# Storing the three pieces of the last output tile through ScalarE's queue

## The chip, the cores and the metric

One core of one Trainium2 chip. The metric is the device time of one execution in microseconds (us). The kernel before takes 906.08 us, the median of 3 runs (905.79 to 906.3). All runs told here are fast, at a granted TensorE clock of 0.998 to 1.000.

## The reference

The program computes `x + s * g` for 2048 rows of 640 columns, in bfloat16. `s` is an attention over the last 512 of 2048 keys with 32 heads of 192, projected back by `wo`; `g` is a gated layer. Cut to what matters:

```python
def reference(A_x, A_k_cache, A_v_cache, A_wq, A_wo, B_x, B_w_gate, B_w_up, B_w_down):
    # ... _A_ref: q = x @ wq, softmax over the last 512 keys, o @ wo
    # ... _B_ref: (sigmoid(x @ w_gate) * (x @ w_up)) @ w_down
    xn = _layernorm(x, axis=-1)
    s = _A_ref(xn, A_k_cache, A_v_cache, A_wq, A_wo)
    g = _silu(_B_ref(xn, B_w_gate, B_w_up, B_w_down))
    return x + s * g
```

## The kernel before

The heads are worked off in groups. In the last group each tile of 128 output rows is finished: a product with the last slice of `wo` in PSUM, a multiply by the gate, an add of everything gathered so far, and a store to HBM. Only this end matters here.

```python
    def finish(ps, gB_sb, t, d0, d1, on_pool=False):
        o_sb = late["fout"].tile([P, D], BF16, name="o_sb")   # a pool of 4 buffers
        d = slice(d0, d1)
        if on_pool:
            tmp = late["tmp"].tile([P, D], F32, name="tmp")
            nc.vector.tensor_tensor(tmp[:, d], ps, gB_sb[:, d], ALU.mult)
            nc.gpsimd.tensor_tensor(o_sb[:, d], tmp[:, d], acc[t][:, d], ALU.add)
        else:
            nc.vector.tensor_tensor(ps, ps, gB_sb[:, d], ALU.mult)
            nc.vector.tensor_tensor(o_sb[:, d], ps, acc[t][:, d], ALU.add)
        nc.sync.dma_start(of[t * P:(t + 1) * P, d], o_sb[:, d])

    def stage_wo(r, i, q):
        # ...
        if r == last and i * TQ + q == 2 * TQ - 1:             # the last tile
            cuts = [0, D // 2, D - P, D]                       # pieces of 320, 192, 128 columns
            for e, (d0, d1) in enumerate(zip(cuts, cuts[1:])):
                ps = ps_all[:, (4, 5, 0)[e], 0:d1 - d0]
                wo_mm(ps, r, i, q, [(d0, d1 - d0)], d0)
                finish(ps, gates[t], t, d0, d1)
            return
        # ... the other tiles; the one before the last is finished with on_pool=True
```

So the add of the tile before the last runs on GpSimd, those of the three pieces on VectorE, and all stores are issued by the SP engine ("sync") in program order.

The softmax here doesn't subtract the row's maximum and nothing guards it: scores larger than these inputs give would overflow.

## Time and profile before

| | us |
|---|---|
| time (median) | 906.08 |
| span of the profiled run | 904.37 |
| last matmul ends | 898.65 |
| VectorE's adds of the pieces a, b, c end | 898.88, 899.55, 900.20 |
| their stores leave SP | 900.03, 900.50, 901.29 |
| their stores have landed | 901.68, 902.06, 903.27 |
| from c's landing to the end | 1.09 |

Three readings are worth learning before the prediction's lines. A store has two times: the issue, which the timeline shows on the sequencer that issues it (`SPq`, `ACTq`), and the landing, when the last of the sixteen DMA engines has reported; the trace records each of the sixteen reports. An instruction's wait is over when its semaphore reaches its value, which the trace also records; an instruction that starts much later than that was held by something else. And the queues in the page tell who issued what:

```profile
q1 hardware_dynamic: 159088, 57.85, 32.2%
q10 hardware_dynamic: 19488, 11.41, 5.3%
q8 instruction: 61, 1.00, 0.5%
q14 instruction: 24, 0.20, 0.1%
```

These are the queue's packets, megabytes and share of the DMA engines' time. q10 holds exactly ScalarE's issues (28 loads of 192 KB and 6 of 960 KB make 11.4 MB), so q1 is SP's; q8 and q14 bring instructions.

### The profile page before, as it was taken

To read this page: it belongs to the slowest core of one execution; us is meant where nothing else is said; L and a number is where in the kernel's file an instruction comes from. 1 tells how busy PE (TensorE), PEld (TensorE's weight loads), DVE (VectorE), ACT (ScalarE), POOL (GpSimd) and SP (SyncE) were. 2 spreads that over 40 slices of the span, in tenths; PEclk is the share of its full clock that TensorE was granted. 3 is DMA by queue.
4 is the path that set the end of the run, shared out by engine and by line. 5 is a ranking of instruction groups with operands and counts; after the bars stand their busy time and mean duration, and the time that the engine had idled before them with its cause. 6 is when DMAs were issued, how large, how long until landed. Compare 5 with 4: busy or idle time off the path is not lost.

```text
span 904.4 us, 18474 instructions
## 1 busy us (share of the span) xinstructions
PE 890.9 (99%) x7711; PEld 530.8 (59%) x7791; DVE 652.3 (72%) x1090; ACT 433.0 (48%) x511; POOL 179.3 (20%) x220
## 2 busy tenths in 40 slices
PE   8999999999999999999999999999999999999997
PEld 5545454556656565656565656565666666666664
DVE  4879956677677866785778677867786678666566
ACT  4323346764247533753375337643764285424240
POOL 0051212780001100110011001100110000002972
PEclk9999999999999999999999999999999999999999
DMA  9993374415544545364626362727293715264744
GB/s 280 271 265 95 97 146 104 119 54 87 86 91 68 135 78 99 60 143 69 109 60 143 62 115 52 151 54 123 36 167 50 126 34 117 48 111 147 155 120 114
DMA packets 188069, 100.38 MB, mean 111 GB/s; under 512 B 156176, under 2 KB 180368, under 8 KB 187984
## 3 DMA queue, kind: packets, MB, share of 16 engines
q1 hardware_dynamic: 159088, 57.85, 32.2%
q0 software_dynamic: 9408, 29.93, 14.0%
q10 hardware_dynamic: 19488, 11.41, 5.3%
q8 instruction: 61, 1.00, 0.5%
q14 instruction: 24, 0.20, 0.1%
HBM read 57.87 MB, written 5.24 MB: 70 GB/s over the span
## 4 chain that ended last, share of the span: by engine, by line
PE 96%; issue 1%; DVE 1%; DMA 1%; ACT 0%; SPq 0%; POOL 0%; DVEq 0%; POOLq 0%
PE ps_all L714 22%; PE ps_all L563 20%; PE ps_all L671 19%; PE ps_all L653 18%; PE ps_all L447 11%; PE ps_all L497 6%; PE ps_all L360 1%; DMA x_sb<-in_A_x_dram 0%; DVE qT L601 0%; ACT E L657 0%; DVE raw L221 0%; DMA out_dram<-o_sb 0%; POOL o_sb L726 0%; SPq L297 0%; DVE stats L324 0%
## 5 line engine op out<-in xcount | busy, mean ns | idle before, releaser
L657 ACT ACTIVATE E<-ps_all 128x1024 bf16<-128x1024 f32 x256 | 252.9, 1022 | 302.8 <-PE ps_all L653 255.5
L714 PE MATMUL ps_all<-wo_g,oT 128*128 128x128 bf16 (+2 forms) x1479 | 225.0, 295 | 3.3
L653 PE MATMUL ps_all<-qT,kT 64*128 64x512 bf16 x1536 | 194.4, 376 | 0.0
L671 PE MATMUL ps_all<-v_sb,E 128*128 128x193 bf16 x2048 | 189.8, 247 | 0.1
L671 PEld LDWEIGHTS <-E 128*128 128x128 bf16 x2048 | 168.6, 98 | 18.7 <-issue 6.8
L714 PEld LDWEIGHTS <-oT 128*128 128x128 bf16 x1542 | 121.5, 98 | 78.3 <-issue 2.1
L584 DVE COPY qp<-ps_all 128x512 f32<-128x512 f32 x150 | 100.7, 688 | 58.5 <-PE ps_all L563 58.4
L601 DVE TENSOR_TENSOR qT<-ps_all,qp 128x512 bf16<-128x512 f32 x165 | 109.6, 687 | 45.7 <-PE ps_all L563 37.4
L653 PEld LDWEIGHTS <-kT 64*128 64x128 bf16 x1536 | 75.3, 94 | 89.4 <-issue 5.2
L678 DVE TENSOR_TENSOR o_st<-ps_all,rden 128x768 bf16<-128x768 f32 x120 | 114.9, 957 | 5.0 <-DMA oT<-o_st 0.9
L202 POOL DMA_DIRECT2D raw<-in_A_wq_dram x80 | 48.5, 611 | 274.0 <-ACT wB L224 237.6
L135 POOL DMA_DIRECT2D k_sb<-in_A_k_cache_dram x32 | 32.7, 1027 | 276.3 <-DVE o_st L678 155.7
L219 ACT ACTIVATE raw<-raw,w_sc 128x1536 f16<-128x1536 bf16 x37 | 58.3, 1575 | 1.4 <-DMA raw<-in_A_wq_dram 0.5
L497 PE MATMUL ps_all<-wd_sb,hT_sb 128*128 128x128 bf16 (+1 forms) x377 | 52.4, 298 | 0.4
L563 PE MATMUL ps_all<-XA,wA 64*128 64x512 f16 x420 | 51.9, 376 | 0.2 <-DVE qp L584 0.2
L563 PE MATMUL ps_all<-XB,wB 64*128 64x512 f16 x420 | 52.0, 376 | 0.0
L563 PE MATMUL ps_all<-X,w 64*128 64x512 bf16 x420 | 51.9, 376 | 0.0
L749 DVE TENSOR_TENSOR acc_lo<-ps_all,acc_lo 128x640 f32<-128x640 f32 x48 | 39.4, 822 | 15.2 <-PE ps_all L714 15.1
L453 DVE TENSOR_TENSOR hT_sb<-ps_all,sig_sb 128x512 bf16<-128x512 f32 x48 | 32.4, 682 | 21.7 <-ACT sig_sb L452 11.4
L677 DVE RECIPROCAL rden<-ps_all 128x4 f32<-128x4 f32 x128 | 23.1, 180 | 33.5 <-PE ps_all L671 32.3
L452 ACT ACTIVATE sig_sb<-ps_all 128x512 bf16<-128x512 f32 x48 | 28.0, 596 | 39.8 <-PE ps_all L447 36.7
L749 DVE TENSOR_TENSOR acc_hi<-ps_all,acc_hi 128x640 f32<-128x640 f32 x48 | 39.3, 818 | 7.8 <-PE ps_all L714 7.8
(118 smaller groups left out, 761.6 us busy)
## 6 DMA issues: line engine op xcount, KB each, us to landing
raw<-in_A_wq_dram POOLq DMA_DIRECT2D x80, 192.0 KB, 3.8
k_sb<-in_A_k_cache_dram POOLq DMA_DIRECT2D x32, 192.0 KB, 5.9
wo_g<-in_A_wo_dram ACTq DMA_DIRECT2D x6, 960.0 KB, 6.8
v_sb<-in_A_v_cache_dram ACTq DMA_DIRECT2D x28, 192.0 KB, 3.7
gB_d<-gB_sb POOLq DMA_DIRECT2D x16, 160.0 KB, 4.2
gBa_sb<-gB_d SPq DMA_DIRECT2D x16, 160.0 KB, 3.8
xa_sb<-in_A_x_dram SPq DMA_DIRECT2D x16, 160.0 KB, 3.8
out_dram<-o_sb SPq DMA_DIRECT2D x15, 160.0 KB, 1.8
```

Of the source, the lines that this page charges most:

```text
L219: nc.scalar.activation(raw.bitcast(F16), raw, AF.Copy, scale=w_up)
L447: nc.tensor.matmul(gu[:, i, :], lhsT=w[:, c, f * P:(f + 1) * P], rhs=xnT[s][:, c, :], start=(c == 0), stop=(c == NCD - 1),)
L497: nc.tensor.matmul(oB_ps[:, d0:d0 + dsz], lhsT=hT_sb[:, f, q * P:(q + 1) * P], rhs=wd_sb[:, f, d0:d0 + dsz], start=(f == 0), stop=(f == NF ...
L563: nc.tensor.matmul(ps_all[:, b, :], lhsT=w(r, c), rhs=x[r, c, :], start=(first and k == 0), stop=(k == len(cs) - 1), skip_group_check=True,)
L584: nc.vector.tensor_copy(dst, part(b))
L601: nc.vector.tensor_tensor(q_out(i, u, pp), part(b), t, ALU.add)
L653: nc.tensor.matmul(ps[:, b, :], lhsT=kT[h, c * PC + j, :], rhs=qT_t[r][i, j][h, pp, :], start=(j == 0), stop=(j == PC - 1),)
L657: nc.scalar.activation(E_t[r, i, pp][:, c, :, :], ps, AF.Exp, scale=scale_qk)
L671: nc.tensor.matmul(o_ps[:, q // 2, q % 2, 0:DH + 1], lhsT=E[:, c, h, q * P:(q + 1) * P], rhs=vt[:, c, 0:DH + 1], start=(c == 0), stop=(c = ...
L678: nc.vector.tensor_tensor(o_st[:, :, h * DH:(h + 1) * DH].rearrange("p (b i) d -> p b i d", b=2), o_ps[:, :, :, 0:DH], rden[:].to_broadcas ...
L714: nc.tensor.matmul(oA[:, d0 - base:d0 - base + dsz], lhsT=oT_t[r, i, pp][:, q * PC + j, :], rhs=wo_t[runs[r][1]][:, cc, d0:d0 + dsz], star ...
L749: nc.vector.tensor_tensor(acc[t][:], oA[:, 0:D], acc[t][:], ALU.add)
```

## The change

Its intent is to let the three last stores leave by a queue that has nothing else to do at the end, instead of standing behind the store of the tile before.

```diff
-    def finish(ps, gB_sb, t, d0, d1, on_pool=False):
+    def finish(ps, gB_sb, t, d0, d1, on_pool=False, queue=nc.sync):
 ...
-        nc.sync.dma_start(of[t * P:(t + 1) * P, d], o_sb[:, d])
+        queue.dma_start(of[t * P:(t + 1) * P, d], o_sb[:, d])
 ...
-                finish(ps, gates[t], t, d0, d1)
+                finish(ps, gates[t], t, d0, d1, queue=nc.scalar)
```

## The prediction

> **What bounds the kernel now.** I read the page first, then the chain that ended last, then the timeline of the last seven microseconds, the waits of the DMA queue's own sequencer there, and the issues with their times to landing.
>
> ```profile
> span 904.4 us, 18474 instructions
> PE 890.9 (99%) x7711; PEld 530.8 (59%) x7791; DVE 652.3 (72%) x1090; ACT 433.0 (48%) x511; POOL 179.3 (20%) x220
> PE 96%; issue 1%; DVE 1%; DMA 1%; ACT 0%; SPq 0%; POOL 0%; DVEq 0%; POOLq 0%
> ...
> out_dram<-o_sb SPq DMA_DIRECT2D x15, 160.0 KB, 1.8
> ```
>
> TensorE is busy for 99% of the span and makes 96% of the chain. Nothing in the change touches it, so the body of 898 us stays as it is. What can move is the end, after the last matmul. There the timeline shows this:
>
> ```profile
> 897.66 0.99 PE L714 MATMUL ps_all<-wo_g,oT 128*128 128x192 bf16 x12
> 898.01 1.54 POOL L726 TENSOR_TENSOR o_sb<-tmp,acc_hi 128x640 bf16<-128x640 f32 x1
> 898.39 0.49 DVE L729 TENSOR_TENSOR o_sb<-ps_all,acc_hi 128x320 bf16<-128x320 f32 x1
> 899.19 0.36 DVE L729 TENSOR_TENSOR o_sb<-ps_all,acc_hi 128x192 bf16<-128x192 f32 x1
> 899.91 0.29 DVE L729 TENSOR_TENSOR o_sb<-ps_all,acc_hi 128x128 bf16<-128x128 f32 x1 [0.16 <-DVE ps_all L728]
> ...
> 897.95 0.33 SPq L730 DMA_DIRECT2D out_dram<-o_sb  x1
> 899.58 0.33 SPq L730 DMA_DIRECT2D out_dram<-o_sb  x1
> 900.03 0.35 SPq L730 DMA_DIRECT2D out_dram<-o_sb  x1
> 900.50 0.39 SPq L730 DMA_DIRECT2D out_dram<-o_sb  x1
> 901.29 0.33 SPq L730 DMA_DIRECT2D out_dram<-o_sb  x1
> ```
>
> First two columns: start and duration in us. TensorE ends at 898.65. Call the three pieces of the last tile a (320 columns), b (192) and c (128). Their adds end at 898.88, 899.55 and 900.20. The stores come out much later: the SP sequencer takes them in program order, so it first waits for GpSimd's add of the tile before (ends 898.01 + 1.54 = 899.55), issues that store at 899.58, and only then a at 900.03, b at 900.50 and c at 901.29. Piece a waits 1.15 us behind a store that it has nothing to do with, b 0.95, c 1.09.
>
> ```profile
> SPq L730 <- POOL o_sb L726: 3.2, 2, 2.0
> SPq L861 <- DMA out_dram<-o_sb: 1.2, 1, 1.2
> ...
> out_dram<-o_sb SPq DMA_DIRECT2D x1, 80.0 KB, 1.6
> out_dram<-o_sb SPq DMA_DIRECT2D x1, 48.0 KB, 1.6
> out_dram<-o_sb SPq DMA_DIRECT2D x1, 32.0 KB, 2.0
> ```
>
> The first line is SP held by GpSimd; the second is the closing wait of the program, 1.2 us, for the landing of c (issue 901.29 + 1.98 = 903.27). From there the closing barrier runs to 904.37: 1.10 us. So the end is: c's add 900.20, 1.09 us of queueing, 1.98 us of transfer, 1.10 us of closing = 904.37.
>
> **What the Trainium skill says.** "DMA: Bandwidth & Descriptors", section "Issuing engines are not separate DMA queues": transfers of all issuing engines run on the same 16 DMA engines, and issuing from several saves only sequencer time, "usually small". The trace agrees so far that sequencer time is all there is to win, but here it is on the path: 1.09 us in front of the last store.
> "Perfetto Trace Analysis", section "DMA Instruction — HWDGE (DVE, Sync)": the descriptor generator is locked for one sequencer at a time, inside the profiled issue. ScalarE's 28 loads of v took 547 ns min and median, 649 at most, though many ran beside a transpose of SP; so sharing cost them 0.1 us at worst.
> "Runtime: NRT & Kernel Launch", section "Instruction fetch mechanics": an engine's instructions come in blocks of 256. I compared every SP record with the moment its semaphores were satisfied. Only two started more than 0.15 us after it: SP's record 79 (0.23 us) and record 335 (0.34 us), exactly 256 apart, each followed 0.6 us later by one 8 KB packet of the instruction queue that took 540 ns. Record 335 is the store of c. So 0.34 of its 1.09 us looks like a block boundary, and the trace agrees with the page.
> The same DMA page, "Anatomy of one DMA — SWDGE (gpsimd) path", puts the fixed cost of a transfer at about 2 us, mostly the write receipt. The trace has 1.57 to 1.98 us for 32 to 160 KB, nearly flat in size; no queue will shorten it.
>
> **The change, part by part.** Removed from SP: three issues with their semaphore waits (six records). Added to ScalarE: the same six, after its last exponential, which ended at 871.0; ScalarE has nothing else to do. On TensorE, VectorE and GpSimd the order of instructions is the same, and each store keeps its waits. Nothing is removed from the data movement.
>
> Piece a: ScalarE can issue it at 898.91 (add's end + 0.03 us, the reaction that SP shows after GpSimd: 899.55 to 899.58). It lands near 900.6, no longer on the path.
> Piece b: add ends 899.55, issue at 899.58, the same instant as SP's store of the tile before. If they exclude each other, one starts up to 0.35 us later.
> Piece c: add ends 900.20. ScalarE is free at 899.58 + 0.39 + 0.06 = 900.03 (or about 900.4 after a collision), so c goes out at 900.23 (900.45). Saved: 901.29 − 900.23 = 1.06 us (0.84).
> Landing of c: 15 of the 16 engines' completions of c had arrived 1.54 us after issue; the last came 0.44 us after them, and the 540 ns instruction packet above was in flight just then, at 901.93 to 902.47. With c's packets at 900.9 to 901.4 I expect no such straggler: lands at 900.23 + 1.54 = 901.77. Saved: another 0.44.
> Closing: SP now reaches its final waits at about 900.0, waits for the tile before (lands 899.58 + 1.79 = 901.37) and meets its block boundary, record 335, as the sixth of the closing waits. So 901.37 + 2 × 0.06 + 0.34 = 901.83 plus one more wait, 901.89, is about the earliest for the wait on c; that takes back 0.12 us. End: 901.89 + 1.10 = 902.99.
>
> Sum: 1.06 + 0.44 − 0.12 = 1.38 us. Taking a third of the possible collision (0.22) off, I predict 1.3 us: 906.08 − 1.3 = 904.8 us, or 0.14%. As the change leaves the 1.7 us between span and measured time alone, the span should be about 903.1.
>
> **The rivals.**
> First: the pieces are hidden behind the tile before, whose store cannot be issued before 899.58 and lands at 901.37. Its end would be at least 901.37 + 1.10 = 902.47, so it caps the gain at 1.9 us. It is not the last one as long as c lands later, which the sum above says by 0.4 us.
> Second: the buffer of c. Its add waited for the landing of the store issued at 897.95 (lands 899.73, add at 899.91). That store stays on SP, so the wait stays, and c's add with it. Were it delayed by traffic of a, now earlier, c would slip; but a's packets start about 0.7 us after issue, at 899.6, when that store's packets are through (seen from 898.7 to 899.3). Cost: under 0.1 us.
> Third: issues from two queues exclude each other or the ScalarE queue is slower. For: both queues issue at 899.58. Against: the same 960 KB load of wo took 377 ns to issue on SP and 374 to 413 on ScalarE, and landings were 5.1 to 6.9 us against 5.4 to 7.7. If each ScalarE store cost 0.4 us more, the gain falls to 0.8 us: 905.3.
> Fourth: the straggler of c is not from the instruction packet but comes with every last store. Then 0.44 us stays and the gain is 0.9 us: 905.2.
> Fifth: a fetch boundary of ScalarE falls on these instructions; that would cost some 0.3 us: 905.1.
>
> **Range and chances.** The bad cases together (collision 0.22, straggler 0.44, boundary 0.3) would leave 0.4 us, 905.7; the cap gives 904.2. The three runs of before spread by 0.5 us, so I take 904.1 to 905.9. Two per cent is 18 us; everything after the last add is 904.37 − 900.20 = 4.2 us, so a gain of 2% is not to be had here, and a loss of 2% would take a transfer ten times slower than any store in the trace. Within 2%: 0.99.
>
> **What would show it right or wrong.** Right: ScalarE's queue shows three stores at about 898.9, 899.6 and 900.2; SP has one store last, at 899.58; VectorE's last add still starts at 899.91; the last landing is at 901.8 to 902.0; the closing barrier is still 1.1 us long; the span is near 903.1. The block boundary is right if c goes out within 0.1 us of its add, and if one of SP's closing waits passes late. Wrong: c issued later than 900.5 (a collision or slow ScalarE queue), c landing 2 us after its issue (the straggler belongs to the last store), or a last add later than 900.2 (buffer). A span that differs before 897 would mean that something other than the tail moved, and no step here accounts for that.

## The result and the profile after

The changed kernel took 904.86 us (median of 6 runs, 904.6 to 905.2); the kernel before, on the same chip, 905.89 us (905.74 to 906.3, 6 runs). The ratio is 0.9988 with a 95% interval of 0.9975 to 1.0001. Ratios here are the mean time of one kernel's fast runs over that of the other's fast runs of the same rounds, so they are not quite the ratio of the medians. This interval just includes 1; the first experiment below narrows that.

The page of the changed kernel:

```profile
span 902.9 us, 18554 instructions
PE 896.0 (99%) x7791; PEld 531.6 (59%) x7791; DVE 653.0 (72%) x1090; ACT 432.9 (48%) x511; POOL 178.8 (20%) x220
q1 hardware_dynamic: 158656, 57.69, 32.5%
q10 hardware_dynamic: 19920, 11.57, 5.5%
PE 21%; DMA 1%; issue 0%; DVE 0%; POOL 0%; DVEq 0%; POOLq 0%
```

Exactly 432 packets went from q1 to q10: three stores of 128 rows, each with sixteen reports. Two lines invite a wrong reading. PE's busy time seems to have risen by 5 us, but its count rose by 80 to 7791, the number of weight loads in both traces: 80 matmul records are missing from the trace of before. And the chain that ended last gives PE 21% instead of 96%: the walk back broke off part-way (the shares add up to about 22%), while PE is busy for 99% of the span as before. Neither is an effect of the change.

The end of the timeline shows the effect (start and duration in us; a, b and c are ScalarE's three):

```profile
899.66 0.29 DVE L729 TENSOR_TENSOR o_sb<-ps_all,acc_hi 128x128 bf16<-128x128 f32 x1 [0.16 <-DVE ps_all L728]
...
898.66 0.37 ACTq L730 DMA_DIRECT2D out_dram<-o_sb  x1
899.33 0.33 SPq L730 DMA_DIRECT2D out_dram<-o_sb  x1
899.33 0.38 ACTq L730 DMA_DIRECT2D out_dram<-o_sb  x1
899.98 0.34 ACTq L730 DMA_DIRECT2D out_dram<-o_sb  x1
```

The waits of SP at the end and the issues to landing:

```profile
SPq L730 <- POOL o_sb L726: 3.2, 2, 2.0
SPq L861 <- DMA out_dram<-o_sb: 1.4, 1, 1.4
...
out_dram<-o_sb ACTq DMA_DIRECT2D x1, 80.0 KB, 2.1
out_dram<-o_sb ACTq DMA_DIRECT2D x1, 48.0 KB, 2.1
out_dram<-o_sb ACTq DMA_DIRECT2D x1, 32.0 KB, 1.6
```

SP still waits 3.2 us for GpSimd (the columns are total, times and longest, in us), but no piece stands behind it any more. a and b take longer to land than before and c less.

In this run the last add comes 0.25 us earlier than in the run of before, and so does the last matmul (898.40 against 898.65). That is drift of the body from run to run, so the end is best measured from a point inside it. I use the tail: from the end of c's multiply on VectorE to the end of the span. It is 4.61 us before and 3.35 us after, 1.26 us less. Term by term, from the end of c's add (what lies between the multiply and that point, a wait of 0.16 us and the add of 0.29, is the same in both):

| from the trace | before | after | gained |
|---|---|---|---|
| c's store leaves, after its add's end | 1.09 | 0.03 | 1.06 |
| c's store lands, after it leaves | 1.98 | 1.61 | 0.37 |
| of it, the 16th report after the 15th | 0.44 | 0.03 | 0.41 |
| from c's landing to the end | 1.09 | 1.26 | −0.17 |
| sum | 4.17 | 2.90 | 1.26 |

### The profile page after: what moved, and what is told of

Read it like the earlier page. It is cut to its first block, busy times and chain, and to the rows that moved or that the text cites. A ratio compares the mean times of both kernels' runs of the same rounds, so it can differ in the third digit from the quotient of the medians.

```text
span 902.9 us, 18554 instructions
## 1 busy us (share of the span) xinstructions
PE 896.0 (99%) x7791; PEld 531.6 (59%) x7791; DVE 653.0 (72%) x1090; ACT 432.9 (48%) x511; POOL 178.8 (20%) x220
## 5 line engine op out<-in xcount | busy, mean ns | idle before, releaser
L714 PE MATMUL ps_all<-wo_g,oT 128*128 128x512 bf16 (+2 forms) x1542 | 228.3, 299 | 0.0
L497 PE MATMUL ps_all<-wd_sb,hT_sb 128*128 128x512 bf16 (+1 forms) x384 | 52.8, 299 | 0.0
```

What stands on the lines that cost most here:

```text
L497: nc.tensor.matmul(oB_ps[:, d0:d0 + dsz], lhsT=hT_sb[:, f, q * P:(q + 1) * P], rhs=wd_sb[:, f, d0:d0 + dsz], start=(f == 0), stop=(f == NF ...
L714: nc.tensor.matmul(oA[:, d0 - base:d0 - base + dsz], lhsT=oT_t[r, i, pp][:, q * PC + j, :], rhs=wo_t[runs[r][1]][:, cc, d0:d0 + dsz], star ...
```

## The experiments

The theory has two halves. First, order: the pieces stood behind a store that waited for GpSimd, and any change of order that lets them pass gains the same; ScalarE's queue has no virtue of its own. Second, blocks: SP's 336th record (numbered 335, counting from 0) starts a new block of instructions, is held for about 0.34 us, and 0.6 us later an 8 KB packet of instructions travels on the DMA engines and delays one report of whatever is moving. In the kernel before that record is the store of c. The rivals: ScalarE's queue is faster; the 0.34 us is a limit on stores in a row; the last report of the last store is always late; or it is all drift.

The first four ran on one chip together, the next four together, and the last pair together, each beside 9 runs of the kernel before (medians 906.03, 906.33 and 906.05). The diffs with `queue=nc.scalar` in a line taken out are against the changed kernel, the others against the kernel before unless the text says otherwise.

**The changed kernel again.** No edit.

> The changed kernel once more, unedited, in five rounds, to narrow the interval that still touched 1.0. I call the tail the time from the end of VectorE's last add to the end of the span: 4.17 us before, 2.90 us in the changed kernel's profile. If the gain is real and lies in the tail: 0.9 to 1.4 us faster than the kernel before (ratio 0.9985 to 0.9990), tail 2.8 to 3.0 us. If it was drift between runs: ratio 0.9995 to 1.0005, and the tail still 2.9.

Measured: 904.7 us (5 runs, 904.63 to 904.92), ratio 0.9987, interval 0.9974 to 0.9999, which leaves 1 out by a hair. The tail is 3.34 us (2.89 from the end of the add). The gain came again, and it lies in the tail.

**Block boundary moved, all stores on SP.**

```diff
-        nc.sync.dma_start(gates[t][:], gB_d[t * P:(t + 1) * P, :])
+        eng = nc.scalar if t in (9, 10) else nc.sync
+        eng.dma_start(gates[t][:], gB_d[t * P:(t + 1) * P, :])
```

> The kernel before with all stores on SP; only two gate loads, some 45 us before the end, go from SP to ScalarE's queue. That takes two records out of SP's program, so that the store of c is SP's record 333 and the block boundary (record 335) falls on a closing wait that waits anyway. Block theory: c is issued 0.75 us after its add instead of 1.09, no 8 KB instruction packet is in flight while it moves, all 16 completions arrive within 1.6 us; tail 3.4 us instead of 4.17, time 0.75 us faster. Rival (the 0.34 us is a limit on a fourth store in a row, and the straggler comes with any last store): tail 4.1 to 4.2 us, time unchanged.

Measured: 905.13 us (5 runs), ratio 0.9991 (0.9977 to 1.0004), tail 3.81 us, 0.80 less than before; from the end of the add 3.36. The stores in the timeline (the tile before, a, b, c), and the time from issue to landing of c:

```profile
899.37 0.33 SPq L731 DMA_DIRECT2D out_dram<-o_sb  x1
899.79 0.38 SPq L731 DMA_DIRECT2D out_dram<-o_sb  x1
900.29 0.38 SPq L731 DMA_DIRECT2D out_dram<-o_sb  x1
900.78 0.37 SPq L731 DMA_DIRECT2D out_dram<-o_sb  x1
...
out_dram<-o_sb SPq DMA_DIRECT2D x1, 32.0 KB, 1.5
```

The four stores are now evenly spaced, where before the last step was 0.80 us, and c lands 1.48 us after issue with the 16th report 0.02 us after the 15th. Record 335 is a closing wait, and it starts 0.34 us after it could. So the hold follows the record number, not the store. The hold and the late report are both gone from c although no store was moved and c is still the fourth in a row and the last: that rules out the limit on stores in a row and the last store that is always late. The interval for the time alone reaches 1; the trace decides here.

**One store moved instead of three.**

```diff
-                finish(ps, gates[t], t, d0, d1, queue=nc.scalar)
+                finish(ps, gates[t], t, d0, d1)
 ...
-            finish(oA[:, 0:D], gates[t], t, 0, D, r == last and (q % 2 == 1 or (i, q) == (1, 2)))
+            queue = nc.scalar if r == last and (i, q) == (1, 2) else nc.sync
+            finish(oA[:, 0:D], gates[t], t, 0, D, r == last and (q % 2 == 1 or (i, q) == (1, 2)), queue)
```

> The kernel before with one store moved instead of three: the store of the tile before the last goes to ScalarE's queue, the three pieces stay on SP. Head-of-line theory (the pieces stood behind a store that waits for GpSimd): the pieces leave SP 0.03 to 0.06 us after their adds, c lands within 1.6 us, the block boundary falls on a closing wait that waits anyway: tail 2.75 us, time 1.2 to 1.5 us faster than before. Rival (ScalarE's queue is the faster one for the pieces): c stays slow on SP, tail 3.3 us or more.

Measured: 904.35 us (5 runs, 904.08 to 904.5), ratio 0.9982 (0.9969 to 0.9994), tail 3.15 us; from the end of the add 2.69.

```profile
898.50 0.33 SPq L730 DMA_DIRECT2D out_dram<-o_sb  x1
899.16 0.33 SPq L730 DMA_DIRECT2D out_dram<-o_sb  x1
899.16 0.38 ACTq L730 DMA_DIRECT2D out_dram<-o_sb  x1
899.82 0.33 SPq L730 DMA_DIRECT2D out_dram<-o_sb  x1
```

The pieces leave SP 0.03 us after their adds. Which of the two parties moves to the other queue does not matter; what matters is that no piece stands behind that store. The tail is 0.2 us shorter than with three stores moved, as SP keeps enough records for its boundary to fall on a wait that is long anyway.

**Only a and b on ScalarE, c on SP.**

```diff
-                finish(ps, gates[t], t, d0, d1, queue=nc.scalar)
+                finish(ps, gates[t], t, d0, d1, queue=nc.sync if e == 2 else nc.scalar)
```

> The changed kernel with only a and b on ScalarE and c back on SP. Head-of-line theory: c leaves SP at once, as the store before it was issued 0.6 us earlier; SP's block boundary moves to a closing wait that waits for the tile before anyway, which gives back the 0.15 us that the changed kernel loses there: tail 2.75 us, 0.1 to 0.2 us less than the changed kernel. Rival (c profits from ScalarE's queue itself): tail 3.2 us or more.

Measured: 904.53 us (5 runs), ratio 0.9985 (0.9972 to 0.9997). c left SP 0.03 us after its add, as expected. But the profiled run's tail is 3.37 us (2.92 from the end of the add), not 0.15 less than with all three moved: c landed 1.79 us after issue. The last report of each of the last four stores was late, that of a by 0.53 us and those of the tile before, b and c by 0.21 each. An 8 KB instruction packet had started at 899.33 and taken 589 ns, just ahead of a's packets; it comes in every one of these traces near this point and is not timed with SP's boundary (whose it is, is told before the table below). The run with one store moved has the same pattern, weaker: 0.56 us in a, 0.08 to 0.15 in the other three. That one DMA engine stayed behind from there on fits these numbers, but the trace does not tell which of the sixteen a packet used, so it is not shown. As a test of order this run agrees; the last 0.15 us it missed.

**Only c on ScalarE.**

```diff
-                finish(ps, gates[t], t, d0, d1, queue=nc.scalar)
+                finish(ps, gates[t], t, d0, d1, queue=nc.scalar if e == 2 else nc.sync)
```

> Only c on ScalarE; a and b stay on SP behind the store of the tile before. Head-of-line theory: c leaves at once and lands 1.6 us after its add, but b is still issued 0.30 us after the last add (as in the kernel before) and lands at +1.85; the closing waits pass b and then c: tail 3.0 us, time 1.1 us faster than before, 0.1 to 0.2 less gain than with all three. SP's block boundary falls on its second closing wait, hidden behind b's landing. Rival (only the last store matters): tail 2.75.

Measured: 905.08 us (4 runs), ratio 0.9987 (0.9973 to 1.0001), tail 3.50 us (3.05 from the end of the add). c left at +0.03 and landed at 901.93; b left at +0.29 and landed at 902.12, and the end hung on it. The order theory's 3.0 holds against the 2.75 of "only the last store matters".

**Four records more on SP.** The boundary is pushed onto the store of a.

```diff
-        nc.sync.dma_start(gates[t][:], gB_d[t * P:(t + 1) * P, :])
+        for c in ((slice(0, D // 2), slice(D // 2, D)) if t in (9, 10, 11, 12) else (slice(0, D),)):
+            nc.sync.dma_start(gates[t][:, c], gB_d[t * P:(t + 1) * P, c])
```

> All stores on SP as in the kernel before; four gate loads some 45 us earlier are cut into two halves each, which puts four more records into SP's program, so that its record 335 is the store of a instead of c. Block theory: a is issued 0.34 us later, b and c queue behind it, so c leaves 1.0 to 1.1 us after its add as before; but the 8 KB instruction packet now flies 0.6 us after a's issue and meets a's or b's packets, not c's: a or b shows a 16th completion 0.3 to 0.5 us behind its 15th, c none: tail 3.7 us, time 0.45 us faster than before. Rival (the straggler comes with the last store whatever the block): c straggles by 0.4 and the tail stays 4.1 to 4.2.

Measured: 906.11 us (5 runs), ratio 0.9998 (0.9985 to 1.001), tail 4.45 us (3.97 from the end of the add). Half right. a was record 335 and was held by 0.36 us; b and c queued behind it, and c left 1.00 us after its add. The late reports moved too: 0.47 us in a and 0.36 in b, only 0.02 in c, while the packet of instructions was in flight at 901.53 to 902.18. But the gain expected from c's punctual landing, 0.45 us, came out as 0.2. The rest is in the closing: 1.34 us from c's landing to the end, against 1.09. SP checks the stores' semaphores one after another in a fixed order, 0.06 us each. The four extra loads turned the assignment of semaphores by four places, so that c's was third instead of seventh in the row, and the other checks came after it.

**The same queue in another order.** No second queue; the store of the tile before is issued after c.

```diff
-        nc.sync.dma_start(of[t * P:(t + 1) * P, d], o_sb[:, d])
+        def store():
+            nc.sync.dma_start(of[t * P:(t + 1) * P, d], o_sb[:, d])
+        if t == 4 * TQ - 2:
+            late["store"] = store
+            return
+        store()
+        if t == 4 * TQ - 1 and d1 == D:
+            late["store"]()
```

> All stores on SP, no second queue: only the order of issue is changed, the store of the tile before the last comes after c. Head-of-line theory: a, b and c leave 0.03 to 0.06 us after their adds and land 1.6 us later; the store of the tile before becomes SP's record 335 and meets the block boundary: issued 0.75 us after the last add instead of 0.42, lands 1.8 to 2.2 us later: tail 3.65 to 4.1 us, time 0.1 to 0.5 us faster than before. Without the boundary it would be 3.3. Rival (the order on SP does not matter, the queue is slow in itself): a, b and c leave later than 0.3 us after their adds.

Measured: 906.27 us (4 runs), ratio 0.9999 (0.9984 to 1.0015), tail 4.56 us (4.11 from the end of the add). The stores of a, b, c and the tile before:

```profile
899.06 0.33 SPq L731 DMA_DIRECT2D out_dram<-o_sb  x1
899.73 0.33 SPq L731 DMA_DIRECT2D out_dram<-o_sb  x1
900.38 0.33 SPq L731 DMA_DIRECT2D out_dram<-o_sb  x1
901.12 0.33 SPq L731 DMA_DIRECT2D out_dram<-o_sb  x1
```

The pieces leave 0.03 us after their adds, on SP. The store put last meets the boundary: 0.34 us of its step are the hold, its 16th report came 0.38 us after the 15th with an instruction packet in flight from 902.05, and it landed 2.25 us after issue. So the order was mended and the gain lost to the block at once. The tail is 0.01 us above the range that was expected, and of the 0.1 to 0.5 us expected in the time 0.1 came, which the interval does not tell from none.

**a and b on ScalarE, c on SP, and a fifth output buffer.** On top of the run with a and b moved, so that c's add does not wait for the store that last used its buffer:

```diff
-            for name, n in ((...), ("fout", 4), (...)):
+            for name, n in ((...), ("fout", 5), (...)):
```

> a and b on ScalarE, c on SP, and five instead of four buffers of the output tile, so that c's add no longer waits for the landing of a store. Counted from the end of c's multiply to the end of the span: 4.61 us before, 3.35 in the changed kernel. Here c's add should start 0.04 us after its multiply instead of 0.16, and the rest be as in the run with one store moved (2.69): 0.04 + 0.29 + 2.69 = 3.02 us; time 1.4 to 1.7 us faster than the kernel before. If the waiting for the buffer was not the cause of the 0.16, it stays and the sum is 3.15 or more.

Measured: 904.56 us (5 runs, 904.51 to 905.02) beside 906.33, ratio 0.9982 (0.997 to 0.9995), tail 3.05 us. c's add began 0.03 us after its multiply instead of 0.16. One thing was not expected: the store issued at 897.94, two tiles before the last, landed only after 2.87 us, and the same store after 2.94 in the next kernel, against 1.78 to 1.87 in every kernel with four buffers and 1.78 in the last kernel below, which has five. With four buffers c's add would have waited for it; with five nothing did. What held it is told, in part, before the table below.

**One store moved and a fifth buffer: a forecast of the block rule.** The last pair combines the best two, and one of them should fail: the fifth buffer gives one of SP's transposes four more waits, two more records, and that puts c back on record 335.

> The kernel with one store moved (that of the tile before the last, to ScalarE), and five output buffers. The fifth buffer brings one of SP's transposes four more waits, hence two more records on SP, as in the run with five buffers before: so the store of c becomes SP's record 335. Block theory, out of sample: c is issued 0.36 us after its add instead of 0.03, and an 8 KB instruction packet flies 0.6 us later. From the end of c's multiply to the end of the span: 0.04 + 0.29 + 0.36 + 1.5 + 1.09 = 3.3 us, 3.7 with a straggler in c; against 3.15 with four buffers: the extra buffer then makes it slower or no faster. Rival (no block rule; a buffer more is a wait less): 3.02 us and 0.1 us faster than with four.

Measured: 905.17 us (5 runs), ratio 0.999 (0.9978 to 1.0003), tail 3.76 us: 0.61 us longer than with four buffers. The last line of its timeline's stores (c), and c's issue to landing:

```profile
899.68 0.29 DVE L729 TENSOR_TENSOR o_sb<-ps_all,acc_hi 128x128 bf16<-128x128 f32 x1
900.21 0.33 SPq L730 DMA_DIRECT2D out_dram<-o_sb  x1
...
out_dram<-o_sb SPq DMA_DIRECT2D x1, 32.0 KB, 2.1
```

c left 0.23 us after its add, not 0.36: the hold of 0.34 us is counted from when SP was ready for the record, before the add ended, so part of it was hidden. Its 16th report was 0.55 us behind the 15th, with an instruction packet in flight at 901.01 to 901.53.

> The same with two gate loads moved to ScalarE's queue, which takes two records back out of SP's program: c is record 333, the boundary falls on a closing wait. Block theory: c issued 0.03 us after its add, from the end of its multiply to the end of the span 0.04 + 0.29 + 2.69 = 3.02 us, 0.3 to 0.7 us shorter than the other kernel of this pair; time 1.4 to 1.8 us under the kernel before. Rival: no difference between the two of this pair.

Its edit is the one of the second experiment on top. Measured: 904.54 us (5 runs), ratio 0.9985 (0.9972 to 0.9999), tail 3.07 us, 0.69 less than its partner:

```profile
899.45 0.29 DVE L730 TENSOR_TENSOR o_sb<-ps_all,acc_hi 128x128 bf16<-128x128 f32 x1
899.77 0.33 SPq L731 DMA_DIRECT2D out_dram<-o_sb  x1
...
out_dram<-o_sb SPq DMA_DIRECT2D x1, 32.0 KB, 1.6
```

Both kernels do the same work at the end; two loads nearly 50 us earlier decide where the block boundary falls.

**How long a block is, and whose the other packet is.** The traces hold more on this than the runs above used, and it corrects one number. SP's record 207, halfway between 79 and 335, started 0.34 us after the record before it ended in all twelve traces, though other waits like it start after some 0.05 us. It then waited 4 us for a semaphore, which hid the hold from a search that looks only at how long after its semaphores a record starts. So the holds are 128 records apart, not 256. The packets agree: SP, ScalarE, VectorE and GpSimd have 351, 748, 1480 and 367 records in the trace of before; one packet in 128 records would make 20 to 24, one in 256 only 9 to 13, and q14 brought 24, of 8 KB each, in each of the twelve traces. The packet near 899.3 fits VectorE's record 1471, the add of b (its multiply in the two kernels whose store of 897.9 was late): it started 0.3 to 0.7 us after that record. In the run with four records more VectorE has five records more as well, its record 1471 is the multiply of a, and the packet came 1.45 us before the end of c's multiply, where in the eleven others it lay between 0.28 us before and 0.03 after.

The traces also show how such a packet makes a report late. In the kernel before, SP's packet ended at 902.47. Of c's 128 row packets 120 had started by 902.37; the other eight, one sixteenth, started one after another from 902.47 on. With four records more SP's packet ended at 902.18, and the last eight rows of a started from 902.18 on; with one store moved and a fifth buffer both were at 901.53 (c). These eight rows behave as one DMA engine's share that had to wait for the packet. (With the order changed the picture is less clean: the packet ended at 902.36, and the last rows of the store are strewn from 902.46 to 902.83.) The late store of 897.9 met VectorE's packet: the last of its sixteen report packets of 4 bytes started where that packet ended, at 899.76 and 899.73 in the two kernels, 0.40 and 0.45 us after the other fifteen. The rest of its delay of 1.09 and 1.15 us stays open.

All of them together; the tail is of one profiled run each, the time is the ratio's distance from 1, times 906 us:

| kernel | tail, us | tail against before | time against before |
|---|---|---|---|
| before | 4.61 | | |
| a, b, c on ScalarE (the change) | 3.35 | −1.26 | −1.1 |
| the change again | 3.34 | −1.27 | −1.2 |
| boundary moved only | 3.81 | −0.80 | −0.8 |
| one store moved | 3.15 | −1.47 | −1.6 |
| a, b on ScalarE | 3.37 | −1.24 | −1.4 |
| c on ScalarE | 3.50 | −1.12 | −1.2 |
| four records more | 4.45 | −0.16 | −0.2 |
| order on SP changed | 4.56 | −0.05 | −0.1 |
| a, b on ScalarE, 5 buffers | 3.05 | −1.56 | −1.6 |
| one store moved, 5 buffers | 3.76 | −0.86 | −0.9 |
| the same, boundary moved | 3.07 | −1.55 | −1.4 |

The two columns agree within 0.2 us throughout, though no single time is told apart from its neighbour by its interval. The version to keep is the one with a single store moved, 904.35 us: none of the others beats it, and neither the fifth buffer nor the moved boundary adds anything measurable to it.

## Why the prediction was right

The predicted 904.8 us met 904.86 (and 904.7), and the mechanism was the one described. That the first number came so close is in part luck: the kernel before took 905.89 us beside it and not 906.08, so the medians differ by 1.03 us where 1.3 was predicted. Point by point:

- The issue of c: 1.06 us predicted, 1.06 measured (from 1.09 to 0.03 us after its add). Moving the boundary alone takes off 0.31 of this, close to the 0.34 told beforehand; the rest is order.
- The straggler: 0.44 us predicted, 0.41 measured. In the changed kernel the late report is in a (0.42 us), where nothing waits for it. The base landing was 0.03 to 0.07 us longer than the 1.54 assumed, so this term gave 0.37.
- The closing: 0.12 us taken back was predicted, 0.17 measured. Record 335 was the sixth closing wait, as told, and was held by 0.28 us beyond b's landing.
- The collision of the two queues (0.22 us, of which a third was taken off): it did not come at the issue. SP's and ScalarE's issues at 899.33 took 332 and 376 ns, and ScalarE's store of a, with no issue of SP beside it, 371. No exclusion is seen; instead the transfers overlapped (both queues' packets run between 900.4 and 900.8), b landed 2.08 us after issue where it took 1.57 before, and the tile before 1.90 instead of 1.79. The latter pushes the closing back by 0.1 us; otherwise nothing waited for them.
- The buffer: c's add kept its wait of 0.16 us, as told. A fifth buffer takes that away.
- The block: the prediction read blocks of 256 records from holds at 79 and 335 and missed the one at 207. The blocks are of 128. Its sum does not suffer, as record 335 is a boundary either way and the changed kernel's SP has no more than 345 records.
- The cap of 1.9 us was never reached; the best tail gains 1.56.

The worked sum of 1.38 us overshot the tail's 1.26 by 0.12: 0.07 in the landing and 0.05 in the closing. The 1.3 us that was stated was closer only because it had been shaded for a collision at the issue that did not come. In the times the gain was 1.1 to 1.2 us.

What stays open: whether a single late DMA engine explains the run with a and b moved, and 0.7 us of the delay of the store of 897.9 in two kernels with five buffers.

## What to carry to other kernels

A store that is ready waits behind any earlier one in the same queue whose producer is late; at the end of a kernel, put the late producer's store into a queue of its own, and it is enough to move that one. Measure such an end from an instruction inside it, not by the whole time, which drifts by nearly as much as the effect (the kernel before took 905.51 to 906.45 us, the gain is 1.2). When an instruction starts later than its semaphores allow, count records: if such holds are a fixed number apart (128 here), adding or removing an unrelated instruction far away moves the hold, and can make a good change look useless (as the new order did here) or a neutral one look good.

## What the Trainium skill lacked or had wrong

- "Runtime: NRT & Kernel Launch", section "Instruction fetch mechanics", has instructions refilled in blocks of 16 KiB, 256 instructions, and calls the cost of crossing a block boundary "mostly hidden". Here only q8's 61 packets are of 16 KB, which fits TensorE's 15,582 matmuls and weight loads (one for 255). The four other engines' records fit q14's 24 packets of 8 KB, one for 128 records, and SP's holds are 128 apart (records 79, 207 and 335, in all twelve traces; at 335 a long wait hid it once). The crossing was not hidden where the queue was on the path: it held SP by 0.21 to 0.36 us.
- The same section does not say that the fetched packet (0.3 to 0.65 us in these traces) delays data moving on the DMA engines at that time: where SP's packet met a store's rows, one of the store's sixteen reports came 0.36 to 0.55 us after the others.
- "Perfetto Trace Analysis", section "DMA Instruction — HWDGE (DVE, Sync)", has the descriptor generator locked for exclusive use. Stores issued by SP and ScalarE within 3 ns took 332 and 376 ns (another pair 333 and 376), against 332 and 371 apart. The longest beside an issue of SP was 475 ns, once (a and b on ScalarE, 5 buffers); SP's own store of c took 511 ns with no issue of ScalarE near it (four records more). No run here shows one of the two waiting for the length of the other's issue.
- No page has the order of the closing checks: SP tests the stores' semaphores one by one at 0.06 us each, so the closing after the last landing took 1.34 us where that store was third in the row and 1.09 where it was seventh.
